# A four-bank burst for the first Fourier stage in a fused S4D and gated-GLU kernel

## The chip, the cores and the metric

The kernel runs on one core of one Trainium2 chip. The metric is device time in microseconds (us). Before the change, three runs gave 742.46, 738.54 and 740.25 us, a median of 740.25 us. One more execution was recorded by the hardware profiler, and all lines of profile and trace below come from that one.

The engines are named as the profile names them: PE is the matrix engine (PEld its weight loads), DVE the vector engine, ACT the scalar engine, POOL the GpSimd engine, SP the engine that here only issues transfers. ACTq and SPq stand for the transfer queues that ACT and SP feed. Every engine works through its own list of instructions in a fixed order.

## The reference, cut to what matters

The input is one sequence of 2048 tokens with 448 channels. After a layer norm, two branches are computed from the same normalized tokens and added to the input:

```
xn = layernorm(x)                                   # x: [1, 2048, 448]
# branch A: a state-space layer as one long convolution
K  = 2 * Re( sum_n C[d,n] * dt[d] * exp(A[d,n] * dt[d] * l) )     # 448 channels, 256 states, l < 2048
yA = irfft( rfft(xn, 4096) * rfft(K, 4096) )[:2048] + xn * D_skip
# branch B: a gated feed-forward layer, 448 -> 1792 -> 448
yB = (sigmoid(xn @ w_gate) * (xn @ w_up)) @ w_down
out = x + yA + yB
```

## The kernel before, in words

Two generators, `conv` (branch A) and `glu` (branch B), emit work in turn. Each `yield` returns a number of units, and the loop at the end of the kernel always continues the generator that has done the smaller share of its total. So the interleaving of the two branches is set by these numbers. After that a scheduler, which simulates a timeline, sets the final order of the instructions on every engine; a smaller change in one place can therefore move instructions elsewhere. `tc.issue_after(i)` holds an instruction back, in that order, until instruction `i` has been placed; `hp` gives priority.

Branch B is done in two halves of 1024 tokens, each half being two blocks of 512 tokens. The 1792 hidden units are cut into 14 tiles of 128, and the tiles into groups of 3, 3, 3, 3 and 2. For each tile and block, `gate` runs 22 matmuls (L693) into two PSUM banks called `gu`: 11 for the gate and 11 for the up projection, because each product of 32-bit numbers is split into high and low parts (`xh`, `xl`, `wh`, `wl`). ACT then takes the tanh (`th`, L701) from the first bank, DVE multiplies it with the second (`hf`, L704), ACT casts (`hh`, L709) and DVE subtracts (`hl`, L711). A new weight tile costs a load on SP (`wraw`), a cast on ACT (`wh`, L743) and a subtraction on DVE (`wl`, L747). When a group of tiles is through, eight output groups `po` (L806) run, one per 128 tokens, and DVE adds each to an accumulator (`acc`, L811). `gu` and `po` share one ring of four PSUM banks: a new `gu` or `po` waits until the bank that was used four places earlier has been read by ACT (`th`) or DVE (`hf`, `acc`).

Branch A first prepares its parameters (`prep`, two halves of 224 channels each: exponentials, reciprocals in pieces L317, arctan, sines, on DVE, ACT and POOL), stores them as phases `ph_d` in device memory, and then builds the convolution kernel in 56 chunks (`kgen`). Each chunk begins on PE with the two matmuls `tr<-sel,ph` (L526), goes through ACT (`S`, L532 to L535) and DVE (`Et`, `Ft`, L586 to L588) and returns to PE (`ko<-Et,Ft`, L600). While chunks are built, branch B fills the engines' free time. The last part, `spectra`, multiplies spectra and transforms back.

The change touches the first Fourier stage of the tokens of the first half. It runs once per pair of token blocks of 128, in `x_spec`, four times in all, between the steps of `prep`. A pair needs four row groups of 32 partitions (g = 0 to 3). For one row group `x_first_stage` runs two matmuls with 32 rows and 64 columns each, one for either block of the pair, into the two halves of one PSUM bank; PE records each such matmul twice. `x_spec` does the four row groups in two steps of two: two row groups go into the two banks of the PSUM tile `tr`, ACT copies both banks to one of three SBUF slots (x1a, x1b, x1c, used in turn; L292), and ACT's queue stores the slot with two transfers (L295). The tiles `tr` (two banks), `ko` and `kp` (one bank each) have one buffer each; `ko` and `kp` are otherwise used by the transposes of the prepared parameters (`turn`, L426) and, later, by the chunks. For the second half of the tokens, another function, `pair_first`, does the same stage in one go over four banks of the `gu` ring.

## Time and profile before

| what | value |
|---|---|
| median of three runs | 740.25 us (738.54 to 742.46) |
| profiled execution, its own time | 735.94 us |
| its span, first to last instruction | 734.2 us |
| mean granted PE clock | 0.978 of full speed |
| busy: PE, DVE, ACT, POOL | 682.4, 557.0, 421.1, 355.9 us |
| `x_spec`: bursts on PE | 8 in the trace, from 42.49 to 79.64 us |
| `prep`: last phase product on DVE (L403) | 107.27 us |
| first chunk on PE (L526) | 127.40 us |

Times in the rows of the trace are counted from the first instruction. A row of the timeline gives start, duration, engine, line, operation, destination and source, shapes and the number of merged instructions; square brackets give how long the engine had been idle and what ended the wait. A table of stretches gives, for each stretch, its length, the busy time of PE, PEld, DVE, ACT and POOL with the number of instructions, the granted PE clock, the busy share of the transfer engines, and GB/s. The profiled execution lies 4.31 us below the median of the runs.

### The profile page before, as it was taken

The page shows a single profiled execution, that of the slowest core. Times are in us where ns is not written, and L with a number is a line of the kernel's source. Part 1 is how long each engine was busy: PE and PEld are TensorE (multiplying, and loading weights), DVE is VectorE, ACT ScalarE, POOL GpSimd, SP SyncE. Part 2 cuts the span into 40 slices and gives each one's busy share as a digit, 9 for nine tenths or more (in the row PEclk, how much of TensorE's full clock was granted, in tenths as well). Part 3 has the DMA queues.
Part 4 walks back from the last instruction along what each step waited for, and adds up shares of the span by engine and source line. Part 5 has one row for each costly group of instructions (what it writes and reads, how often), then busy time and mean ns, then how long its engine had stood idle before and what let it go on. Part 6 is the DMA issues. An engine that isn't in the chain of part 4 may idle for free.

```text
span 734.2 us, 19242 instructions
## 1 busy us (share of the span) xinstructions
PE 682.4 (93%) x7780; PEld 532.7 (73%) x7780; DVE 557.0 (76%) x776; ACT 421.1 (57%) x650; POOL 355.9 (48%) x423
## 2 busy tenths in 40 slices
PE   2898998999999899999999999998999999999995
PEld 2666787877877687565888877887877778776784
DVE  5899995699978989768667987977975555565543
ACT  3646483578677868797487787677652222323320
POOL 2110055684975986548467498486855001441002
PEclk9999999999999999699999999999999999999998
DMA  9946445444324635345972332332158999999845
GB/s 208 225 131 179 113 135 176 134 138 168 96 89 135 221 86 155 98 127 174 278 191 88 111 108 80 100 104 80 45 163 272 257 253 241 266 262 221 199 118 160
DMA packets 102984, 117.24 MB, mean 160 GB/s; under 512 B 13232, under 2 KB 90864, under 8 KB 102896
## 3 DMA queue, kind: packets, MB, share of 16 engines
q1 hardware_dynamic: 78736, 91.87, 45.3%
q10 hardware_dynamic: 21584, 18.24, 9.6%
q0 software_dynamic: 2576, 5.90, 3.0%
q8 instruction: 61, 1.00, 0.6%
q14 instruction: 27, 0.22, 0.1%
HBM read 72.13 MB, written 43.84 MB: 158 GB/s over the span
## 4 chain that ended last, share of the span: by engine, by line
PE 55%; DVE 17%; ACT 8%; DMA 8%; issue 5%; POOL 4%; SPq 2%; ACTq 1%; DVEq 0%; POOLq 0%
PE gu L693 23%; PE po L806 13%; PE sp L888 5%; PE ko L600 5%; PE pv L915 3%; PE tr L526 3%; DVE Ft L588 2%; DVE Et L587 2%; ACT S L535 2%; DVE Et L586 2%; DVE pm L440 2%; ACT S L532 1%; DMA sx<-x_d 1%; ACT S L533 1%; DMA tb<-in_c_tab_dram 1%
## 5 line engine op out<-in xcount | busy, mean ns | idle before, releaser
L504 POOL TENSOR_TENSOR me<-me,pm 128x32 f32<-128x32 f32 (+1 forms) x168 | 137.5, 819 | 114.8 <-DVE Et L587 102.9
L504 POOL TENSOR_TENSOR mf<-mf,pm 128x64 f32<-128x64 f32 (+1 forms) x112 | 113.8, 1016 | 5.2
L693 PE MATMUL gu<-xh,wh 128*128 128x512 f32 x336 | 100.2, 404 | 2.6 <-DVE acc L811 1.1
L693 PE MATMUL gu<-xh,wl 128*128 128x512 f32 x336 | 97.8, 396 | 0.0
L693 PE MATMUL gu<-xl,wh 128*128 128x512 f32 x336 | 96.2, 394 | 0.0
L586 DVE TENSOR_TENSOR Et<-me,S 128x1024 f32<-128x1024 f32 x56 | 80.1, 1430 | 18.1 <-ACT S L535 17.0
L587 DVE TENSOR_TENSOR Et<-me,S 128x1024 f32<-128x1024 f32 x56 | 78.9, 1410 | 15.4 <-ACT me L517 12.0
L806 PE MATMUL po<-dh,hh 128*128 128x448 f32 x224 | 85.1, 380 | 3.7 <-DVE acc L811 3.0
L588 DVE TENSOR_TENSOR Ft<-mf,S 128x1024 f32<-128x1024 f32 x56 | 79.3, 1416 | 5.5 <-ACT S L535 4.5
L806 PE MATMUL po<-dl,hh 128*128 128x448 f32 x224 | 83.2, 371 | 0.0
L806 PE MATMUL po<-dh,hl 128*128 128x448 f32 x224 | 82.4, 369 | 0.0
L693 PEld LDWEIGHTS gu<-xh,wh 128*128 128x128 f32 x336 | 61.2, 190 | 23.5 <-issue 6.1
L600 PEld LDWEIGHTS ko<-Et,Ft 128*32 128x32 f32 x3584 | 54.5, 111 | 32.3 <-DVE Ft L588 13.8
L532 ACT ACTIVATE S<-tr 128x1024 f32<-128x1024 f32 x56 | 57.7, 1030 | 33.2 <-PE tr L526 31.5
L600 PE MATMUL ko<-Et,Ft 128*32 128x64 f32 x3584 | 64.9, 223 | 12.4 <-DVE Ft L588 12.4
L693 PEld LDWEIGHTS gu<-xh,wl 128*128 128x128 f32 x336 | 63.7, 190 | 14.7 <-DVE ys L257 0.7
L693 PEld LDWEIGHTS gu<-xl,wh 128*128 128x128 f32 x336 | 63.8, 190 | 14.3 <-issue 0.7
L709 ACT CAST hh<-hf 128x512 fp32r<-128x512 f32 x56 | 34.9, 623 | 62.7 <-DVE hf L704 62.6
L704 DVE SCALAR_TENSOR_TENSOR hf<-th,gu 128x512 f32<-128x512 f32 x56 | 38.2, 682 | 40.4 <-PE gu L693 34.7
L701 ACT ACTIVATE th<-gu 128x512 f32<-128x512 f32 x56 | 33.6, 601 | 59.6 <-PE gu L693 46.1
L535 ACT ACTIVATE S<-S,hpi 128x1024 f32<-128x1024 f32 x56 | 65.6, 1172 | 0.0
L811 DVE SCALAR_TENSOR_TENSOR acc<-po,acc 128x448 f32<-128x448 f32 x80 | 48.1, 617 | 19.4 <-PE po L806 19.4
(198 smaller groups left out, 1295.1 us busy)
## 6 DMA issues: line engine op xcount, KB each, us to landing
sk_d<-sk ACTq DMA_DIRECT2D x14, 512.0 KB
sx<-x_d SPq DMA_DIRECT2D x32, 224.0 KB
skl<-sk_d SPq DMA_DIRECT2D x16, 448.0 KB
vp<-v_d SPq DMA_DIRECT2D x16, 448.0 KB
v_d<-vt SPq DMA_DIRECT2D x62, 112.0 KB
ph<-ph_d SPq DMA_DIRECT2D x224, 24.0 KB
wt_d<-wh SPq DMA_DIRECT2D x9, 512.0 KB
wt_d<-wl SPq DMA_DIRECT2D x9, 512.0 KB
```

What stands on the lines that cost most here:

```text
L504: ins = nc.gpsimd.tensor_tensor(m[:, :, w + a : 2 * w : n], m[:, :, a:w:n], par(base + i).unsqueeze(2).to_broadcast([128, 4 * DC, w // n]) ...
L532: nc.scalar.activation(rows(cs), pv, AF.Abs)
L535: sins[:] = [nc.scalar.activation(cs, cs, AF.Sin, scale=-TWO_PI, bias=hpi)]
L586: v.tensor_tensor(Et[:, :, :, 32:64], two(me[:, :, 32:64]), S[:, 1::-1], ALU.mult)
L587: v.tensor_tensor(Et[:, :, :, 0:32], two(me[:, :, 0:32]), S[:, 1:3, :, ::-1], ALU.mult)
L588: fts[:] = [v.tensor_tensor(Ft, two(mf), S[:, 3:5], ALU.mult)]
L600: mm = nc.tensor.matmul(ko[32 * j : 32 * j + 32, sl], Ft[:, cc, DC * h + 4 * q + j], Et[:, cc, DC * h + 4 * q + j], start=(k == 0), stop=( ...
L693: glu_mm[:] = [nc.tensor.matmul(ps, a_, b_, start=(n == 0), stop=(n == len(mm) - 1))]
L704: marks[1] = v.scalar_tensor_tensor(hf, th, 1.0, pgu[1], ALU.add, ALU.mult)
L806: glu_mm[:] = [nc.tensor.matmul(po, a_[:, bs], w_, start=(n == 0), stop=(n == 3 * fc - 1))]
L811: v.scalar_tensor_tensor(acc[:, b], po, 0.5, acc[:, b], ALU.mult, ALU.add)
L888: mm = nc.tensor.matmul(to, tb[:kk, t, 64 * c : 64 * c + 64], rhs, start=True, stop=True, skip_group_check=True,)
```

## The change

`x_spec` now takes two slots at once and runs all four row groups in one burst: the first two into the two banks of `tr` as before, the third into `ko`, the fourth into `kp`. One copy moves the two banks of `tr` to the first slot; two copies of half the size move `ko` and `kp` to the two halves of the second slot. The four stores follow. The generator yields once, with twice the units, so that its total is unchanged. The slots are taken in the same turn: pairs (a, b), (c, a), (b, c), (a, b).

```
 def x_spec(xn, b0):
+    x1s_ = []
+    for _ in range(2):
+        x1s_.append(slots[("x1a", "x1b", "x1c")[x1s[0] % 3]])
+        x1s[0] += 1
+    ps = psc[-1].tile([128, 2, 512], F32, name="tr", bufs=1)
+    kk = [psc[-1].tile([128, 512], F32, name=n, bufs=1) for n in ("ko", "kp")]
+    with tc.issue_after(glu_mm[0].ins):
+        for j in range(4):
+            x_first_stage((ps[:, j] if j < 2 else kk[j - 2])[:, :D], xn, j)
+    nc.scalar.copy(x1s_[0], ps[:, :, :D])
+    for j in range(2):
+        nc.scalar.copy(x1s_[1][:, j], kk[j][:, :D])
     for p in range(2):
-        x1 = slots[("x1a", "x1b", "x1c")[x1s[0] % 3]]
-        x1s[0] += 1
-        ps = psc[-1].tile([128, 2, 512], F32, name="tr", bufs=1)
-        with tc.issue_after(glu_mm[0].ins):
-            for j in range(2):
-                x_first_stage(ps[:, j, :D], xn, 2 * p + j)
-        nc.scalar.copy(x1, ps[:, :, :D])
         for i in range(2):
             r = row(b0 + i, 2 * p)
-            nc.scalar.dma_start(x1_d[:, r : r + 9 : 8], x1[64 * i : 64 * i + 64])
-        yield WX
+            nc.scalar.dma_start(x1_d[:, r : r + 9 : 8], x1s_[p][64 * i : 64 * i + 64])
+    yield 2 * WX
```

The lines behind `x_spec` move down by five, so that L693, L806, L811, L317 and L526 of the profile are L698, L811, L816, L322 and L531 of the changed kernel. The scheduler then places instructions differently at three places that matter here. In the lists below, a row is a line, an operation, its destination and source, a shape and a count.

The first place is PE, from the first burst to the second (`tr`, `ko` and `kp` are the PSUM banks; `gu` are the matmuls of branch B's gates). Before:

```order
L281 MATMUL tr<-xn_117,wx 64x448 x4
L693 MATMUL gu<-xh,wh 128x512 x3
L693 MATMUL gu<-xr,wh 128x512
L693 MATMUL gu<-xh,wl 128x512 x3
L693 MATMUL gu<-xr,wl 128x512
L693 MATMUL gu<-xl,wh 128x512 x3
L693 MATMUL gu<-xh,wh 128x512 x3
L693 MATMUL gu<-xr,wh 128x512
L693 MATMUL gu<-xh,wh 128x512 x3
L693 MATMUL gu<-xr,wh 128x512
L281 MATMUL tr<-xn_117,wx 64x448 x4
```

These two bursts carry four row groups, with 19 gate matmuls between them. On the same engine, at the same place, now:

```order
L281 MATMUL tr<-xn_117,wx 64x448 x4
L281 MATMUL ko<-xn_117,wx 64x448 x2
L281 MATMUL kp<-xn_117,wx 64x448 x2
L698 MATMUL gu<-xh,wh 128x512 x3
L698 MATMUL gu<-xr,wh 128x512
L698 MATMUL gu<-xh,wl 128x512 x3
L698 MATMUL gu<-xr,wl 128x512
L698 MATMUL gu<-xl,wh 128x512 x3
L698 MATMUL gu<-xh,wh 128x512 x3
L698 MATMUL gu<-xr,wh 128x512
L698 MATMUL gu<-xh,wh 128x512
L281 MATMUL tr<-xn_117,wx 64x448 x4
```

One burst now holds all four row groups, and the next pair's burst follows after 16 gate matmuls.

The second place is DVE, in the first output groups of branch B: `acc` are their eight additions, of which the fifth and later ones stand here, and `pl`, `a`, `w` and `ex` belong to `prep`. Before:

```order
L412 TENSOR_TENSOR a_377<-a_377,b_378 112x512
L317 RECIPROCAL pl<-pl 112x128 x4
L259 TENSOR_TENSOR z<-ys 128x8
L811 SCALAR_TENSOR_TENSOR acc<-po,acc 128x448 x2
L412 TENSOR_TENSOR a_389<-a_389,b_390 112x512
L317 RECIPROCAL pl<-pl 112x128 x4
L377 SCALAR_TENSOR_TENSOR w_392<-ci,w_392 112x512
L811 SCALAR_TENSOR_TENSOR acc<-po,acc 128x448
```

The fifth addition stands behind four of the eight reciprocal pieces. On the same engine now:

```order
L259 TENSOR_TENSOR z<-ys 128x8
L382 SCALAR_TENSOR_TENSOR w_380<-ci,w_380 112x512
L417 TENSOR_TENSOR a_377<-a_377,b_378 112x512
L322 RECIPROCAL pl<-pl 112x128 x8
L816 SCALAR_TENSOR_TENSOR acc<-po,acc 128x448 x2
L417 TENSOR_TENSOR a_389<-a_389,b_390 112x512
L260 SCALAR_TENSOR_TENSOR z<-z,ve 128x8
L816 SCALAR_TENSOR_TENSOR acc<-po,acc 128x448 x2
```

Now it stands behind all eight pieces, and nothing else ahead of it has been removed.

The third place is PE, where the first chunk begins (`po` are the output groups of branch B's second group of tiles, 72 matmuls in all). Before:

```order
L806 MATMUL po<-dh,hl 128x448
L806 MATMUL po<-dh,hh 128x448
L806 MATMUL po<-dl,hh 128x448
L806 MATMUL po<-dh,hl 128x448
L806 MATMUL po<-dh,hh 128x448
L526 MATMUL tr<-sel,ph_1095 128x512 x2
```

At that point 264 gate matmuls and 112 output matmuls have been issued, 40 of them from the second group of tiles. On the same engine now:

```order
L698 MATMUL gu<-xl,wh 128x512 x3
L811 MATMUL po<-dh,hh 128x448
L811 MATMUL po<-dl,hh 128x448
L811 MATMUL po<-dh,hl 128x448
L811 MATMUL po<-dh,hh 128x448
L811 MATMUL po<-dl,hh 128x448
L811 MATMUL po<-dh,hl 128x448
L811 MATMUL po<-dh,hh 128x448
L811 MATMUL po<-dl,hh 128x448
L531 MATMUL tr<-sel,ph_1103 128x512 x2
```

The first chunk now comes after 264 gate matmuls and 80 output matmuls: 8 from the second group instead of 40. From the third chunk on, the same number of branch B's matmuls stands ahead of a chunk as before, up to shifts of a few matmuls, and of 35 at the thirtieth chunk.

## The prediction

> **What bounds the kernel now.** I first read the page's busy times, then the table of stretches around the change, then the timeline for who waits for whom. The first row is the page's engine line, the others are stretches (length, then busy time of PE, PEld, DVE, ACT, POOL).
>
> ```profile
> PE 682.4 (93%) x7780; PEld 532.7 (73%) x7780; DVE 557.0 (76%) x776; ACT 421.1 (57%) x650; POOL 355.9 (48%) x423
> ...
> 52.00:62.50 10.50, 9.48 (x54) 5.72 (x52) 10.50 (x15) 3.31 (x5) 1.62 (x1) 1.00 0.82 233
> 62.50:73.00 10.50, 9.11 (x46) 7.07 (x42) 10.50 (x22) 9.51 (x14) 0.00 (x0) 0.84 0.57 159
> 73.00:83.50 10.50, 9.64 (x52) 6.98 (x52) 10.50 (x21) 7.13 (x12) 0.20 (x1) 1.00 0.42 103
> 83.50:99.00 15.50, 15.46 (x70) 12.81 (x71) 15.50 (x30) 6.82 (x14) 1.16 (x1) 1.00 0.23 71
> 99.00:111.00 12.00, 12.00 (x59) 9.95 (x58) 11.53 (x14) 9.43 (x20) 11.71 (x5) 1.00 0.73 210
> 111.00:127.00 16.00, 13.04 (x61) 11.30 (x61) 7.98 (x14) 4.46 (x9) 7.55 (x14) 0.95 0.62 190
> 127.00:147.00 20.00, 20.00 (x146) 16.62 (x145) 12.64 (x18) 10.80 (x15) 14.13 (x19) 0.96 0.39 126
> 147.00:167.00 20.00, 19.84 (x206) 16.02 (x205) 18.38 (x17) 16.10 (x24) 16.44 (x17) 1.00 0.48 164
> 167.00:187.00 20.00, 17.59 (x313) 13.96 (x312) 19.03 (x26) 15.36 (x23) 10.24 (x13) 1.00 0.50 159
> 187.00:207.00 20.00, 19.75 (x270) 16.61 (x269) 16.75 (x15) 12.98 (x19) 19.15 (x19) 1.00 0.24 67
> 207.00:247.00 40.00, 34.82 (x553) 27.26 (x554) 35.54 (x38) 32.20 (x48) 25.55 (x31) 0.97 0.45 144
> ```
>
> Over the whole span PE is the bound (93%). But from 52 to 99 us, where the changed stage runs, DVE has no idle time at all, while PE stands still for 1.02, 1.39 and 0.86 us. There DVE, not PE, sets when things happen. From 127 to 167 PE is full; at 167 to 187 it idles 2.41 us, at 207 to 247 another 5.18.
>
> **The bursts on PE.** A burst of 8 records (two row groups), and bursts of 12 and 4 records of the same stage in the second half:
>
> ```profile
> 41.72 0.84 PE L693 MATMUL gu<-xl,wh 128*128 128x512 f32 x3
> 42.49 0.98 PE L281 MATMUL tr<-xn,wx 32*64 32x448 f32 x8
> 43.40 0.96 PE L693 MATMUL gu<-xh,wh 128*128 128x512 f32 x3
> 44.20 0.40 PE L693 MATMUL gu<-xr,wh 128*128 128x512 f32 x1
> ...
> 319.69 0.99 PE L281 MATMUL gu<-xt,wx 32*64 32x448 f32 x12
> 320.61 0.73 PE L526 MATMUL tr<-sel,ph 128*128 128x512 f32 x2
> 321.42 0.97 PE L281 MATMUL gu<-xt,wx 32*64 32x448 f32 x4
> ```
>
> 4, 8 and 12 records all take 0.97 to 0.99 us, so row groups run side by side, and I take 16 records at 0.98 too (bounds: 0.98, and 1.96 if the fourth row group does not join). A burst costs about 1.1 us: 0.91 from 42.49 to 43.40, 0.09 to 0.12 ahead of it (three matmuls of 0.227 after 41.72 end at 42.40), and the next three matmuls start their successor 0.80 instead of 0.68 later. Four bursts fewer are 4.4 us of PE, at the worst 0. Three of the eight lie after the wait at 63.26, and in the new order none.
>
> **What holds PE instead.** Waits of PE on DVE, and the DVE rows that end them:
>
> ```profile
> 62.52 0.69 DVE L704 SCALAR_TENSOR_TENSOR hf<-th,gu 128x512 f32<-128x512 f32 x1
> 63.26 0.47 PE L806 MATMUL po<-dh,hh 128*128 128x448 f32 x1 [0.71 <-DVE hf L704]
> ...
> 72.97 0.98 PE L281 MATMUL tr<-xn,wx 32*64 32x448 f32 x8 [0.68 <-ACT x1c L292]
> ...
> 79.54 3.40 DVE L317 RECIPROCAL pl<-pl 112x128 f32<-112x128 f32 x4
> 82.28 0.37 PE L806 MATMUL po<-dh,hl 128*128 128x448 f32 x1
> 82.86 1.16 DVE L811 SCALAR_TENSOR_TENSOR acc<-po,acc 128x448 f32<-128x448 f32 x2
> 83.54 0.73 PE L693 MATMUL gu<-xh,wh 128*128 128x512 f32 x2 [0.90 <-DVE acc L811]
> 84.52 3.40 DVE L317 RECIPROCAL pl<-pl 112x128 f32<-112x128 f32 x4
> ```
>
> At 63.26 PE waits for the bank that `hf` frees. DVE's work ahead of that `hf` is the same now but for one operation on 8 elements per partition, so PE gets there 3 us earlier and waits 3 us longer: nothing gained. At 83.54 the first gate of the next group of tiles waits for the bank of the fifth `acc`. In the new order four more reciprocal pieces stand ahead of that `acc` and nothing fewer. DVE has no idle time there to lose, so it ends 3.40 us later (84.52 row), and the gate starts at 86.94. It cannot be earlier unless DVE works faster; it can be later by what ACT adds, below. PE, 4.0 us ahead by three bursts of 1.1 and the 0.68 us that it waited for a copy at 72.97, then stands still for about 0.90 + 4.0 + 3.4 = 8.3 us instead of 0.90.
>
> **The clock.** What PE's clock did after waits:
>
> ```profile
> 64.00:67.00 3.00, 3.00 (x9) 2.67 (x8) 3.00 (x7) 2.79 (x4) 0.00 (x0) 0.50 0.43 127
> 125.70:128.60 2.90, 2.86 (x7) 2.48 (x8) 2.87 (x5) 1.14 (x2) 2.66 (x4) 0.50 0.20 56
> ```
>
> After the waits around 62 and before 125.70, PE ran about 3 us at half the clock, a loss of 1.5 us each; after the 0.90 us at 83.54 it did not (1.00 in both stretches there). With 8.3 us I take 1.5 us, bounds 0 and 1.5. The Trainium skill ("TensorE: Matmul & The Clock Gate", Part 1) says that the clock falls to half after an idle window of about 3.4 us and comes back after as much work. By that page the loss would be 1.7 us, an estimate from its window, and by its rule the shorter waits here should have cost nothing; the row at 64.00 disagrees on the latter. Gates thus run 4.9 us late: 3.4 + 1.5.
>
> **Copies, stores, slots.** One copy of 896 columns and, from the second half, two of 448:
>
> ```profile
> 43.54 0.91 ACT L292 COPY x1ab<-tr 128x896 f32<-128x896 f32 x1 [1.72 <-PE tr L281]
> 321.87 1.00 ACT L675 COPY x<-gu 128x448 f32<-128x448 f32 x2
> 44.48 0.68 ACTq L295 DMA_DIRECT2D x_d<-x1ab  x1
> 49.00:50.00 1.00, 1.00 (x5) 0.82 (x6) 1.00 (x3) 0.88 (x1) 0.00 (x0) 1.00 0.09 26
> L858 SPq DMA_DIRECT2D sx<-x_d x16: 580/612/1456, 532.1 to 677.6; - x16
> ```
>
> Four times 0.09 us more on ACT, hidden: ACT is busy 3.31 of 10.50 us at 52 to 62.5 and nearly full only at 62.5 to 73, where it could push `acc` back by at most some 1 us. The sixteen stores are the same and are read from 532 us on. New is that a copy can overwrite a slot whose stores were issued just before. The first stores, issued from 44.48 on, were through by 49 (transfer share 0.09 in that stretch), so such a copy waits up to some 4.5 us; the cast of tile 3's weights that is queued behind it on ACT is first needed by the gate at 83.54, so I cost it at nothing.
>
> **Where the first chunk starts.** The end of the gates and the first chunk:
>
> ```profile
> 115.32 0.36 PE L806 MATMUL po<-dh,hh 128*128 128x448 f32 x1
> 115.30:122.40 7.10, 7.10 (x36) 6.57 (x35) 1.78 (x6) 0.00 (x0) 1.57 (x6) 1.00 0.77 231
> 121.00 6.83 SPq L476 DMA_DIRECT2D ph<-ph_d  x16
> 125.74 0.74 PE L806 MATMUL po<-dh,hh 128*128 128x448 f32 x1 [2.96 <-DVE acc L811]
> 127.40 1.05 PE L526 MATMUL tr<-sel,ph 128*128 128x512 f32 x2
> ```
>
> Gates that ended at 115.32 now end at 120.2. Eight output matmuls (7.10/36 = 0.20 us each) bring PE to 121.8, and there it stands, in order, at the first chunk, which needs the loads of `ph`. These come at best 2.7 us earlier than before, since two `hf` and two `hl` of about 0.68 us fewer stand ahead of `prep`'s last operation on DVE, and at worst not earlier, because on SP they are queued behind the stores of tile 6, whose weights now load later. So the chunk starts between 124.7 and 127.4; I take 126.0. PE then still owes the 32 output matmuls that it had done by 127.40: 6.4 us. It is behind by 126.0 + 6.4 - 127.4 = 5.0 us, bounds 3.7 and 6.4.
>
> **What is given back.** From 127 to 167 PE is full, so it stays behind. At 167 to 187 its 2.41 us of idle time are waits for the chunk's chain on ACT and DVE, which now started 1.4 us earlier; a PE that is late finds the data ready. I take all of it, and nothing of the 5.18 us at 207 to 247, where DVE is busy 35.54 of 40 us, with work that also follows PE (bounds 0 and 7.6 in all). Sum: 3.4 + 1.5, then 5.0 at the first chunk, less 2.4: +2.6 us. Against the profiled execution, 735.94 becomes 738.5; against the median, which lies 4.31 above it, 740.25 becomes 742.8.
>
> **The rivals.** First, slower: nothing is given back, since chunks and gates are tied by one order on PE and all shift together. Then +5 to +6.4 us, 745.2 to 746.6. For it speaks that PE is full for 40 us after the first chunk; it decides if PE still idles some 2.4 us in the stretch that was 167 to 187. Second, faster: the lateness is regained entirely at 167 to 247, whose 7.6 us of idle time exceed it, and the earlier chunks (up to 2.7 us) shift the chain that ends last there. Then 737.5, or with the saved 4.4 us of PE all coming out 735.9. Against it, that chain also holds `hf` and `acc`, which follow PE. Third, the change doesn't do what it says: the four-bank burst takes twice as long. PE has some 8 us to spare at that place, so the time would be the forecast's, 742.8, within the same case.
>
> **How the numbers follow.** The forecast, with an end 0.5 to 3.7 us above the median before: 0.45. Nothing given back, or more lost: 0.37. Regained: 0.18, of which 0.03 end within 0.5%. The burst of twice the length (under 0.05) is part of the first. About 0.5% (3.7 us) is what a measurement of this kernel can tell from no change. So faster 0.15, same 0.48, slower 0.37. The likeliest case alone runs from 740.7 to 744.0; the range that leaves out 2 in 10 runs from 736.8, near the saved PE time coming out, to 748.0, which is 6.4 us late plus another half-clock stretch of 1.5.
>
> **What would show it.** Right: four bursts of 16 records of about 1 us; DVE still without idle time to 99 us; the gate of 83.54 at 87 or a little later behind a wait of some 8 us for `acc`, then half clock; PE waiting at the first chunk near 126. Given back: less than 1 us of PE idle where it had 2.41. Wrong: if that `acc` comes before 85 us, or if the chunks from 200 us on run earlier than before.

## The result, and the profile after

The changed kernel took 735.59 us (median of nine runs, 729.01 to 737.56) where the kernel before took 738.83 us in the same comparison (nine runs, 736.31 to 744.70). The ratio is 0.993, with a 95% interval of 0.9903 to 0.9957: it is 0.7% faster. (It is not the quotient of these two medians, which is 0.9956. Ratios below leave out disturbed runs, which are two of *rows1*, at 744.24 and 745.42 us, and one of the kernel before, at 748.66.) The prediction was 742.8 us, 2.6 us slower.

The profiled execution of the changed kernel took 737.56 us, its span is 735.7 us and its mean granted clock 0.974. So it is the longest of the nine, and 1.6 us longer than the profiled execution before; where that comes from is part of what follows. First the page's engine line and the table of stretches, both of the changed kernel, with the columns of the prediction's first fence. The row at 86.60 stands for a stretch of half clock, those from 280.60 on for places that the prediction did not speak of.

```profile
PE 680.4 (92%) x7780; PEld 535.5 (73%) x7780; DVE 560.1 (76%) x776; ACT 421.1 (57%) x654; POOL 360.6 (49%) x423
...
52.00:62.50 10.50, 9.08 (x63) 5.79 (x61) 10.50 (x17) 5.00 (x9) 2.26 (x2) 1.00 0.80 231
62.50:73.00 10.50, 8.84 (x30) 7.66 (x30) 10.23 (x21) 8.80 (x14) 0.00 (x0) 0.67 0.68 172
73.00:83.50 10.50, 7.57 (x36) 6.68 (x36) 10.50 (x20) 5.96 (x12) 0.00 (x0) 1.00 0.24 68
83.50:99.00 15.50, 11.54 (x41) 9.27 (x42) 15.07 (x32) 5.66 (x13) 1.61 (x2) 0.78 0.21 67
111.00:127.00 16.00, 16.00 (x77) 13.69 (x76) 8.81 (x17) 8.28 (x15) 9.09 (x16) 1.00 0.49 154
147.00:167.00 20.00, 19.88 (x206) 15.93 (x205) 15.85 (x16) 15.08 (x22) 9.03 (x11) 1.00 0.54 179
167.00:187.00 20.00, 19.85 (x325) 16.21 (x324) 19.90 (x26) 17.36 (x26) 13.04 (x14) 1.00 0.47 147
207.00:247.00 40.00, 34.99 (x615) 27.70 (x617) 36.71 (x39) 33.96 (x51) 32.16 (x32) 1.00 0.48 151
280.60:383.60 103.00, 97.05 (x1372) 68.72 (x1371) 80.49 (x96) 79.78 (x129) 64.22 (x81) 0.97 0.59 174
648.00:656.00 8.00, 5.33 (x78) 3.15 (x75) 7.93 (x12) 0.53 (x1) 4.25 (x4) 0.82 1.08 274
...
86.60:93.40 6.80, 5.94 (x14) 4.69 (x15) 6.80 (x19) 0.84 (x2) 0.00 (x0) 0.50 0.00 0
```

Up to 99 us PE stands for 1.42, 1.66, 2.93 and 3.96 us in the first four stretches, 10.0 us where it stood 3.3 before, and in two of them its clock is at half for a part. At 111 to 127 it does better than before: 16.00 us busy instead of 13.04, at full clock. At 167 to 187 the 2.41 us of idle time are down to 0.15. At 648 to 656 there is a new hole of 2.67 us.

The same two kernels in the time at which PE reaches the same instruction (this table is worked out from both traces by pairing equal matmuls in order, and counts the changed kernel less the kernel before; where chunks and branch B's work have moved against each other, between 147 and 285 us, the row names what is paired):

| place, by the clock of before | PE, us |
|---|---|
| end of the gates (115.32, now 122.02) | +6.7 |
| next gate behind the output groups (134.97, now 138.17) | +3.2 |
| 140 to 147 | +2.0 |
| 187 to 200, output groups | -0.5 |
| 285 to 300 | -2.6 |
| 384 to 480 | -4.2 |
| 490 to 648 | -3.9 |
| from 660 | +1.3 |

So the change is late by 6.7 us, is 3.9 us ahead by 490 us, and in this one execution loses 5.2 us at 650. The first part of the story is told by the timeline of the changed kernel: a burst, the waits of PE on DVE, and the first chunk.

```profile
42.71 0.60 PE L281 MATMUL tr<-xn,wx 32*64 32x448 f32 x4
42.75 0.59 PE L281 MATMUL kp<-xn,wx 32*64 32x448 f32 x2
...
43.17 0.54 PE L281 MATMUL kp<-xn,wx 32*64 32x448 f32 x2
...
64.16 0.74 PE L811 MATMUL po<-dh,hh 128*128 128x448 f32 x1 [3.07 <-DVE hf L709]
...
80.30 6.62 DVE L322 RECIPROCAL pl<-pl 112x128 f32<-112x128 f32 x8
86.85 1.09 DVE L816 SCALAR_TENSOR_TENSOR acc<-po,acc 128x448 f32<-128x448 f32 x2
...
87.46 1.65 PE L698 MATMUL gu<-xh,wh 128*128 128x512 f32 x3 [6.08 <-DVE acc L816]
...
112.49 1.11 SPq L633 DMA_DIRECT2D wraw<-in_B_w_up_dram  x2
115.37 1.05 ACT L748 CAST wh<-wraw 128x1024 fp32r<-128x1024 f32 x1 [4.75 <-DMA wraw<-in_B_w_up_dram]
116.45 1.23 DVE L752 TENSOR_TENSOR wl<-wraw,wh 128x1024 fp32r<-128x1024 f32 x1 [3.89 <-DMA rd<-in_B_w_down_dram]
118.12 7.82 SPq L481 DMA_DIRECT2D ph<-ph_d  x16
122.02 0.36 PE L811 MATMUL po<-dh,hh 128*128 128x448 f32 x1
123.64 0.63 PE L531 MATMUL tr<-sel,ph 128*128 128x512 f32 x2
```

The burst of four row groups takes 1.00 us (43.17 + 0.54 - 42.71). The first gate of the next group of tiles comes at 87.46, behind all eight reciprocal pieces, and the gates end 6.7 us late. But the first chunk stands at 123.64 with no wait before it: it comes 3.76 us earlier than before. Three more profiles whose PE order is the same here (*again*, *wl_dve* and *wl_pieces*, below) have it at 123.73 to 124.63, each with a wait of 0.96 to 1.48 us for ACT's `hh` just ahead of it. In *again*:

```profile
123.00 0.47 PE L811 MATMUL po<-dh,hh 128*128 128x448 f32 x1 [1.48 <-ACT hh L714]
123.73 0.90 PE L531 MATMUL tr<-sel,ph 128*128 128x512 f32 x2
```

The kernel before, in the same 15 us:

```profile
118.74 1.54 SPq L628 DMA_DIRECT2D wraw<-in_B_w_up_dram  x2
...
122.65 1.04 ACT L743 CAST wh<-wraw 128x1024 fp32r<-128x1024 f32 x1 [8.53 <-DMA wraw<-in_B_w_up_dram]
123.73 1.22 DVE L747 TENSOR_TENSOR wl<-wraw,wh 128x1024 fp32r<-128x1024 f32 x1 [6.54 <-DMA ph<-ph_d]
125.07 0.62 DVE L811 SCALAR_TENSOR_TENSOR acc<-po,acc 128x448 f32<-128x448 f32 x1
```

The wait of 2.96 us that the prediction quotes at 125.74 is named for `acc`. But DVE had stood idle for 6.54 us, at the subtraction `wl` of tile 7, whose weights had been loaded by SP as late as 118.74, behind the stores of `ph_d`; the `acc` that PE needed stood behind that `wl`. In the changed order SP issues this load between the stores, the last piece at 112.49, the cast and `wl` come 7.28 us earlier, and the wait for `acc` is gone, with its half clock.

### The profile page after: what moved, and what is told of

The parts are those of the page before. It is cut to its first block, busy times and chain, and to the rows that moved or that the text cites. A ratio compares the mean times of both kernels' runs of the same rounds, so it can differ in the third digit from the quotient of the medians.

```text
span 735.7 us, 19244 instructions
## 1 busy us (share of the span) xinstructions
PE 680.4 (92%) x7780; PEld 535.5 (73%) x7780; DVE 560.1 (76%) x776; ACT 421.1 (57%) x654; POOL 360.6 (49%) x423
## 4 chain that ended last, share of the span: by engine, by line
PE 63%; DVE 13%; DMA 7%; ACT 7%; issue 4%; SPq 3%; POOL 1%; ACTq 1%; POOLq 0%; DVEq 0%
PE gu L698 29%; PE po L811 11%; PE sp L893 7%; PE ko L605 5%; PE pv L920 4%; PE tr L531 3%; DVE Et L591 2%; DVE Ft L593 2%; DVE Et L592 2%; SPq L633 1%; ACT S L540 1%; ACT S L538 1%; DVE acc L816 1%; SPq L481 1%; DMA t<-in_c_t_dram 1%
## 5 line engine op out<-in xcount | busy, mean ns | idle before, releaser
L509 POOL TENSOR_TENSOR me<-me,pm 128x32 f32<-128x32 f32 (+1 forms) x168 | 140.3, 835 | 107.4 <-DVE Et L592 96.3
L509 POOL TENSOR_TENSOR mf<-mf,pm 128x64 f32<-128x64 f32 (+1 forms) x112 | 118.2, 1056 | 4.7
L698 PE MATMUL gu<-xh,wh 128*128 128x512 f32 x336 | 102.3, 412 | 7.0 <-DVE acc L816 6.1
L698 PE MATMUL gu<-xh,wl 128*128 128x512 f32 x336 | 98.9, 402 | 0.0
L698 PE MATMUL gu<-xl,wh 128*128 128x512 f32 x336 | 97.5, 396 | 0.0
L591 DVE TENSOR_TENSOR Et<-me,S 128x1024 f32<-128x1024 f32 x56 | 82.8, 1479 | 12.5 <-ACT S L540 10.8
L592 DVE TENSOR_TENSOR Et<-me,S 128x1024 f32<-128x1024 f32 x56 | 79.4, 1417 | 12.3 <-ACT me L522 9.6
L811 PE MATMUL po<-dh,hh 128*128 128x448 f32 x224 | 85.0, 380 | 3.9 <-DVE hf L709 3.1
L698 PEld LDWEIGHTS gu<-xh,wh 128*128 128x128 f32 x336 | 63.2, 195 | 28.9 <-DVE acc L816 6.5
L811 PE MATMUL po<-dl,hh 128*128 128x448 f32 x224 | 83.0, 371 | 0.0
L811 PE MATMUL po<-dh,hl 128*128 128x448 f32 x224 | 82.0, 369 | 0.0
L593 DVE TENSOR_TENSOR Ft<-mf,S 128x1024 f32<-128x1024 f32 x56 | 76.8, 1372 | 5.2 <-ACT S L540 2.7
L698 PEld LDWEIGHTS gu<-xh,wl 128*128 128x128 f32 x336 | 65.1, 194 | 15.2 <-DVE pl L316 0.7
L698 PEld LDWEIGHTS gu<-xl,wh 128*128 128x128 f32 x336 | 64.5, 192 | 14.0
L816 DVE SCALAR_TENSOR_TENSOR acc<-po,acc 128x448 f32<-128x448 f32 x80 | 48.0, 614 | 21.7 <-PE po L811 21.7
```

The lines of the kernel that those rows point to most:

```text
L509: ins = nc.gpsimd.tensor_tensor(m[:, :, w + a : 2 * w : n], m[:, :, a:w:n], par(base + i).unsqueeze(2).to_broadcast([128, 4 * DC, w // n]) ...
L591: v.tensor_tensor(Et[:, :, :, 32:64], two(me[:, :, 32:64]), S[:, 1::-1], ALU.mult)
L592: v.tensor_tensor(Et[:, :, :, 0:32], two(me[:, :, 0:32]), S[:, 1:3, :, ::-1], ALU.mult)
L593: fts[:] = [v.tensor_tensor(Ft, two(mf), S[:, 3:5], ALU.mult)]
L698: glu_mm[:] = [nc.tensor.matmul(ps, a_, b_, start=(n == 0), stop=(n == len(mm) - 1))]
L811: glu_mm[:] = [nc.tensor.matmul(po, a_[:, bs], w_, start=(n == 0), stop=(n == 3 * fc - 1))]
```

## The experiments

Three explanations of the gain were set against each other: that the PE time saved by the bursts comes out in the end (Theory A of the expectations), and its rivals, that it is the wait removed at the first chunk (Theory B), or the different order further on (Theory C; in the expectations of *first_four* and *second_four* Theory B stands for the order behind the stage). The diffs are against the changed kernel or the kernel before, as named.

### Is it the saved PE time?

**again**: the changed kernel, whose generator yields its units in two steps again. The order on all engines is the same.

```
-        yield 2 * WX
+        yield WX; yield WX
```

> The changed kernel with its one yield of 2*WX written as two of WX; every engine's order of instructions is the same as in the changed kernel. It gives a second profile of that order. The first profile of it (735.7 us of span) was 4.2 us ahead of the old kernel from 400 us on, 3.9 us ahead at 648, and lost 5.2 us between 648 and 662, where a DVE addition of 0.39 us took 2.43 us beside POOL's wl subtraction, PE waited 2.67 us for it and then ran at half clock for 6.8 us. If this collision is a matter of the moment at which a weight load lands, some profiles lack it: then the span is near 730 us and PE has no wait of over 1 us between 640 and 660. If it belongs to the order, it is there again, with a span near 735. Median of the times in both cases 735.6, within 1.5.

736.11 us (733.29 to 738.79), ratio 0.996 (0.9935 to 0.9985). The gain is there with the units returned either way. Its profile is 4.2 us ahead by 480 us, 3.3 at 648 us, and has no hole at 650. (The opposite, one yield of twice the units in the kernel before, is the run *old_again* below.)

**rows2** and **rows1**: the changed kernel, with the four matmul pairs of a burst put on two row groups of PE, or on one, so that they cannot run side by side. In both, all banks but the first hold another row group's product. The edit of *rows2*; in *rows1* the map is `lambda g: 0`:

```
-    def x_first_stage(to, xn, g):
-        s = slice(32 * g, 32 * g + 32)
+    def x_first_stage(to, xn, g, m=lambda g: g):
+        s = slice(32 * m(g), 32 * m(g) + 32)
...
-                x_first_stage((ps[:, j] if j < 2 else kk[j - 2])[:, :D], xn, j)
+                x_first_stage((ps[:, j] if j < 2 else kk[j - 2])[:, :D], xn, j, lambda g: g // 2)
```

> The changed kernel, but the first two row groups of a burst both use row group 0 and the last two row group 1 (token data of a wrong group go into two of four banks, so the computation is changed there). Order of instructions the same on all engines. Matmuls of one row group run one after the other, so a burst should take about 2 us instead of 0.94, four bursts some 4 us more: the PE time that the change saved is put back, and nothing else. Theory A, the gain is PE's saved time: 735.6 + 4 = 739.6. Theory B, the gain comes from what moved on the other queues (the weights of the tile ahead of the first chunk landing 6 us earlier, so that the wait of 2.96 us at 125.74 and its half clock are gone): 735.6, since the waits of PE of 3.07 us (at 64.16) and 6.08 us (at 87.46) take up the 4 us.

> As the run with two row groups, but all four banks of a burst use row group 0 (the computation is changed in three of four banks). A burst of 16 records should take about 4 us, four of them 12 us more than in the changed kernel. Theory A: 735.6 + 12 = 747.6. Theory B: the two waits of 3.07 and 6.08 us take up 9 of the 12 us, 735.6 to 738.6, and the gates still start near 87.5, behind the fifth acc.

Beside *again*, in the same comparison, neither is slower by more than the intervals: 736.19 us, ratio 0.9956 (0.9925 to 0.9986), and 736.66 us, ratio 0.9959 (0.9932 to 0.9986). The timeline of *rows1*, a burst and PE's wait for `acc`:

```profile
40.89 1.72 PE L281 MATMUL tr<-xn,wx 32*64 32x448 f32 x8
42.45 0.92 PE L281 MATMUL ko<-xn,wx 32*64 32x448 f32 x4
43.20 0.92 PE L281 MATMUL kp<-xn,wx 32*64 32x448 f32 x4
...
90.22 1.65 PE L698 MATMUL gu<-xh,wh 128*128 128x512 f32 x3 [6.07 <-DVE acc L816]
```

A burst takes 3.23 us there (40.89 to 44.12), so the four cost 8.9 us more PE time (4 x 2.23) than the changed kernel's, twice what the change had saved. The gate that was expected near 87.5 starts at 90.22. At 648 us *rows1* is 1.7 us ahead of the kernel before, 2.2 behind the changed one. By these two profiles a us of burst on PE costs a quarter of a us, 2.2 of 8.9. This is a rough estimate, since the profiles of the changed kernel, *again*, *wl_dve* and *wl_pieces* lie 2.9 to 5.3 us ahead there with the same bursts. Theory A, which asked for 747.6 us, falls: of 4.4 us saved, some 1 us can come out.

**first_four** and **second_four**: four-bank bursts for the first two pairs alone, or for the last two alone; the others go through the old function, here `x_spec2`. The edit of *first_four*; *second_four* has `n == 3`:

```
-                            yield from x_spec([xns[n - 2][:, b + i] for i in range(2)], 4 * (n - 2) + b)
+                            yield from (x_spec if n == 2 else x_spec2)([xns[n - 2][:, b + i] for i in range(2)], 4 * (n - 2) + b)
```

> The burst over four banks for the first four token blocks alone; the second four run as in the old kernel, in two bursts over two banks. Two bursts fewer instead of four: 2.2 us of PE saved. PE's order from its 545th matmul on (about 145 us) is that of the changed kernel but for three rows. Theory A (what comes out is PE time saved): half the gain, 737.4 against 739.1 and 735.9. Theory B (what comes out is the new order of the work behind the stage): the whole gain, 735.9, with the half-clock stretch near 296 us of 6.8 us that the changed order has in all three profiles so far.

> The burst over four banks for the second four token blocks alone. Again 2.2 us of PE saved, but PE's order from 145 to about 285 us is that of the old kernel, and from there to 360 us a third one. Theory A: half the gain, 737.4. Theory B: no gain from 145 to 285 us, where the changed order gained 3 us against the old one; about 738.5, unless the third order behind 285 us has its own gain or loss, of 1.7 us for every half-clock stretch of 3.4 us more or less than the 13.65 us of the old one.

*first_four*: 735.25 us, ratio 0.9953 (0.9929 to 0.9977), with two bursts saved instead of four: the whole gain and not half of it, as Theory B of its expectation had it. *second_four*: 736.39 us, ratio 0.9972 (0.9945 to 1.0000). In its trace the third and fourth bank of a burst were placed apart from the first two, so that it has eight bursts as before and saves no PE time in them; it is 2.9 us ahead at 126 us all the same, and 4.4 at 383. That agrees with the row-group runs.

### Is it the wait at the first chunk?

**load_first**: the kernel before, with one weight load given priority. It was meant for tile 7 and moved tile 6's.

```
-                            raw, rd = raws.pop() if raws else (w_load(f), None)
+                            with hp(HP if f == 6 else 0):
+                                raw, rd = raws.pop() if raws else (w_load(f), None)
```

> The old kernel with one thing moved: the loads of the weights of tile 6 have a higher priority and are issued on SP ahead of the last ph_d stores instead of behind them. Bursts and banks as before. In the old profile these loads went out from 115.61 on, their cast came at 122.65, DVE stood still for 6.54 us until 123.73, and PE waited 2.96 us at 125.74 and ran at half clock until 128.6. Theory B: the load goes out some 3 us earlier, the cast comes near 119 to 120, PE's wait and its half clock (1.4 us) are gone, and the time falls by 2 to 4.4 us, to 734.4 to 737 against 738.8. Theory A, only the PE time of the bursts counts: no change, 738.8, since other waits take the place of this one.

738.08 us, ratio 0.9978 (0.9952 to 1.0004). Tile 7's load was still late, but on DVE the `acc` came to stand ahead of the waiting `wl`: PE's wait for `acc` at 125 was gone, two shorter ones of 0.35 and 1.15 us came, and PE was 2.5 us ahead at 133 us. By 343 us 0.9 were left, at 490 to 648 us nothing.

**tile7_act**: the kernel before, with tile 7's weights loaded by ACT's queue, past the stores on SP.

```
-                            raw, rd = raws.pop() if raws else (w_load(f), None)
+                            raw, rd = raws.pop() if raws else (w_load(f, eng=nc.scalar if f == 7 else nc.sync), None)
```

> The old kernel with the weights of tile 7 (those loaded from 115.61 us on in its profile; the run before that moved a load had moved tile 6's) loaded through ACT's queue instead of SP's, where they stood behind the last ph_d stores. Their buffer is free at 109.4, so they can go out some 5 us earlier. PE's order is the old one but for three matmuls. Theory B (step 5 of the prediction failed because PE's wait at 125.74 hung on this load): the cast comes near 117 to 119 instead of 122.65, the DVE wait of 6.54 us shrinks to 1 to 3 us, the PE wait of 2.96 us and the half clock at 125 are gone, and at 134 us PE is 2 to 4 us ahead of the old profile. The time: of that lead some 2 us were left at 285 us in the two kernels with the old order that had it, so 736.5 to 738 against 738.5. If the lead at 134 is below 1 us, the wait hung on something else (the loads of ph, from 121.0).

737.76 us, ratio 0.9973 (0.9946 to 1.0001). This kernel waits at the first chunk, for the load of `ph`, instead of for `acc`:

```profile
124.56 0.70 PE L526 MATMUL tr<-sel,ph 128*128 128x512 f32 x2 [1.53 <-DMA ph<-ph_d]
```

2.96 us of wait and 1.5 us of half clock went, 1.53 us came: 2.9 us by the sum, 2.6 us by the pairing of matmuls, the same from 133 to 260 us. That is as much as the changed kernel has at 285 us, had from the old bursts by moving one load, but the changed kernel gets there in another way, as the text behind *old_again* shows. Behind 341 us 0.95 us of it were left.

**old_again**: the kernel before with one yield of twice the units; the order is that of before.

```
-            yield WX
+        yield 2 * WX
```

> The old kernel with its yield of WX behind each of the two bursts written as 2*WX; the order of instructions is the same on every engine. A second profile of the old order: if the 13.65 us of half clock from 296 us on belong to the order, they are there again within 3.4 us (the changed order had 6.8 there in six profiles, with 3.4 more at 329 in four of these), and so are the wait of 2.96 us of PE at 125.74 and the one of DVE ahead of it. Median 738.5, within 1.5.

739.17 us, ratio 0.9974 (0.9948 to 1.0000); in its profile PE waits 2.93 us for `acc` at 125.42, DVE 6.53 us for tile 7's cast, as before. The wait belongs to the old order, not to one execution.

The removed wait can't be the whole gain: the changed kernel is still 2.0 us late at 140 us and 2.6 us ahead by 285 to 300. From 147 to 285 us, eight kernels have one and the same order on PE, matmul for matmul (the changed kernel, *again*, *rows1*, *rows2*, *first_four*, and *wl_dve*, *wl_pieces* and *late_old* below), and the ten others that of before, but for four matmuls in one of them. By the same pairing, from 140 to 147 until 285 to 300 us, the eight regain 4.6 to 6.3 us on the kernel before, whether PE is 1.8 us late at 140 us or, in *late_old*, 21.8. The nine others range from 2.3 us lost to 1.4 us gained. So this part of the gain belongs to the changed order; it needs neither saved PE time nor a first chunk that is early by the clock (127.24 us in *rows1*, 138.60 in *late_old*). What in that order brings it is not shown.

### What lies between 285 and 383 us?

In this stretch *tile7_act* lost 1.8 us of its lead and *load_first* 1, while the changed kernel gained some 1.4. From the 20th to the 33rd `Ft` row (280.6 to 383.6 us before), the six profiles whose order there is that of before take 102.9 to 106.4 us, mean 104.4 (the kernel before, old_again, load_first, tile7_act, and late_old and wl_pieces_old below). Eight kernels with four-bank bursts, whose order there is another, take 99.8 to 102.3 us, mean 101.1 (the changed kernel, again, rows1, rows2, first_four, second_four, and wl_dve and wl_pieces below). These lengths are worked out from the traces. The stretch of the kernel before, and a row of its timeline:

```profile
280.60:383.60 103.00, 98.27 (x1365) 68.64 (x1364) 78.80 (x96) 79.04 (x126) 63.20 (x80) 0.93 0.61 172
...
314.09 0.41 PE L212 MATMUL gu<-ident,xt 128*64 128x128 f32 x2 [0.91 <-DVE xl L222]
```

The clock is 0.93 where the changed kernel has 0.97: half clock for 13.7 us, after for 6.8. PE waits at 314.09 at a transpose of tokens of the second half (L212) for a DVE operation, in *old_again* 2.17 us. In the order before, that transpose stands ahead of a chunk and the `Ft` matmuls (L600) right behind it; in the changed order a whole gate (310.37 to 312.9) stands there, and PE doesn't wait.

**late_old**: the changed kernel with each four-bank burst done twice, so that no PE time is saved.

```
-            for j in range(4):
+            for j in (0, 1, 2, 3) * 2:
                 x_first_stage((ps[:, j] if j < 2 else kk[j - 2])[:, :D], xn, j)
```

> The changed kernel with every burst of 16 records done twice, so that PE's time is again that of the old kernel (the second burst computes the same data once more). Its order is that of the changed kernel from about 145 to 285 us and that of the old one from there on. Theory C, the gain is made between 285 and 325 us, where the changed order stood at half clock for 6.8 instead of 13.65 us: the time is 738.5 to 739. Theory B without C, the gain is made before 285 us: 736 to 736.7. In the trace: lead over the old kernel at 280 us 1 to 3 us as in the changed order, and whether it grows by the 3.4 us of the clock until 325 us.

756.16 us, ratio 1.025 (1.0216 to 1.0285): a miss as a test of the early part, since the scheduler made an early order of its own, in which PE waits 3.30 us for a copy, 4.83 and 2.91 at two more places and 9.52 us for an `acc` at 99.73. From 278 us on its order is that of before, and it stays 16.2 us late there, 16.1 at the end of the stretch. With the old late order nothing is gained in the stretch, however late PE comes.

**turn_late** and **both_waits**: the kernel before, with the transposes of two pairs moved back; *both_waits* has the load of *tile7_act* as well.

```
-            for b in range(nb):
+            with hp(-HP if nb == 2 and k == 3 and o0 == 256 else 0):
+                for b in range(nb):
...
```

> The old kernel with the two bursts over two banks, but the last transposes (64 columns) of the pairs 10 and 14 without their raised priority, so that PE comes to them behind the matmuls of the next chunk instead of ahead of them. In the old order PE waits there, near 313 us, for DVE's xl (0.91, 2.17, 2.12, 2.66, 3.48 us in five profiles); in the changed order these transposes stand later and there is no wait. Between the 20th and the 33rd Ft row that DVE shows (280.6 and 383.6 us in the old profile) six profiles of the old order took 102.9 to 106.4 us, on the mean 104.4, and eight of other orders 99.8 to 102.3, on the mean 101.1. Theory C, a good half of the change's gain is this later order: the stretch takes 100 to 102.3 here too, and the time falls by some 2 to 3.5 us, to 735.5 to 737.5 against 739. If the stretch still takes 103 us or more, the wait near 313 only hid another one.

> The old kernel and its eight bursts, with both moves: tile 7's weights loaded through ACT's queue (PE 2.58 us ahead at 134 us when it was alone) and the 64-column transposes of the pairs 10 and 14 later. If the change's gain consists of these two waits and not of the PE time of its bursts, the old bursts have it too: lead over the old profile 2 to 3 us at 280, 4 to 6 us at 383, and a time of 734 to 736 against 739. If a part hangs on the bursts themselves, it stays above 737.

Both missed. 742.42 us, ratio 1.0042 (1.0017 to 1.0068), and 738.95 us, ratio 1.0003 (0.9979 to 1.0028). The wait at the transpose went and a longer one stood behind it, in *turn_late*:

```profile
316.00 0.42 PE L601 MATMUL ko<-Et,Ft 128*32 128x64 f32 x2 [3.05 <-DVE Ft L589]
```

The stretch took 109.2 us in *turn_late* and 108.0 in *both_waits*, with some 20 us of half clock in either.

**gate_between** and **gate_elsewhere**: the kernel before, with one gate of branch B given priority, so that six of its matmuls stand between chunk and `Ft` matmuls, or a gate that doesn't come to stand there. The edit of *gate_between*; *gate_elsewhere* has `n_ == 1`:

```
-            with tc.issue_after(order[0].ins) if order else nullcontext():
+            with tc.issue_after(order[0].ins) if order else nullcontext(), (hp(HP) if soon == i else nullcontext()):
...
-                    yield from gate(ws[f - f0], xq[2 * half + t], hs[t], between, half == 0 and (f, t) == (1, 0))
+                    yield from gate(ws[f - f0], xq[2 * half + t], hs[t], between, half == 0 and (f, t) == (1, 0), 1 if cross and n_ == 2 else None)
```

> The kernel before, with one of branch B's gates of the group in which the second half begins (third tile of the group, second block) placed with priority, so that 6 gate matmuls stand on PE between the matmuls that open a chunk and the Ft matmuls that follow, near 313 us. Theory: it is the gate at that place, there in the changed order and not in the order before, that covers PE's wait near 313 us; then the stretch from the 20th to the 33rd Ft row takes 101 to 102.5 us where the old order took 103 to 106, the half-clock time there falls to 7 us or less, and the time is some 2 us shorter (ratio near 0.997). Rival: the wait depends on more than that gate (the earlier start of everything from 125 us on, or where the 64-column transposes stand); then the stretch stays at 103 us or more and the ratio at 1.00 or above. Moving the gate also moves POOL's work on the second half, which could lengthen the stretch by itself.

> The same move, with priority for the gate of the second tile instead of the third, so that no gate comes to stand between the chunk and the Ft matmuls near 313 us. Theory (the covering gate): the stretch from the 20th to the 33rd Ft row takes 104 to 109 us, ratio 1.00 or above. Rival (any earlier gate does it): 101 to 102.5 us, as with the other gate.

741.57 us, ratio 1.002 (0.9995 to 1.0045), stretch 103.6 us; and 744.38 us, ratio 1.005 (1.0029 to 1.0071), stretch 108.3 us. In *gate_between* the gate stands where it should, and PE waits all the same:

```profile
316.87 0.52 PE L600 MATMUL ko<-Et,Ft 128*32 128x64 f32 x18 [0.80 <-DVE Ft L588]
318.25 0.41 PE L212 MATMUL gu<-ident,xt 128*64 128x128 f32 x2 [0.85 <-DVE xl L222]
```

So one gate at that place is not the cause. Which part of the changed order shortens the stretch stays open. The stretch is short in all eight profiles with a new order there (six have one and the same, *first_four* and *second_four* variants of it), and no single move of the old order brought it.

### What is the hole at 650 us?

The changed kernel at its new hole (`wl` is the second half's weight subtraction, on POOL; `yy` and `pd` belong to `spectra`, and both inputs of L907 lie in SBUF):

```profile
648.43 1.04 POOL L758 CAST wh<-wraw 128x1024 fp32r<-128x1024 f32 x1 [6.20 <-PE sp L893]
...
649.55 2.37 POOL L759 TENSOR_TENSOR wl<-wraw,wh 128x1024 fp32r<-128x1024 f32 x1
649.74 2.43 DVE L907 TENSOR_TENSOR yy<-pd 128x224 f32<-128x224 f32 x1
...
653.38 1.72 PE L955 MATMUL pv<-vp,wf 64*32 64x224 f32 x16 [2.67 <-DVE pd L905]
...
653.99 0.38 DVE L907 TENSOR_TENSOR yy<-pd 128x224 f32<-128x224 f32 x1
```

The same DVE operation takes 0.38 us at 653.99 and 2.43 us beside POOL's subtraction, and ends 0.25 us after it. PE, two operations further, waits 2.67 us, and then runs 6.8 us at half clock. The rule of the Trainium skill ("SBUF — State Buffer", "Who interferes with whom") is that a DVE instruction with two inputs in SBUF contends with a GpSimd instruction that reads SBUF, and it calls this contention an exclusive lock; these rows agree, with a DVE operation that lasts as long as POOL's. Three more profiles have this hole or one of 0.76 us (*rows2*, *second_four*, *first_four*), *again* and *rows1* have none. It depends on when POOL's subtraction falls: in *again* it starts at 651.12, behind the first of these DVE operations (0.39 us), and holds the second (2.04 us), for which PE doesn't wait. In the kernel before, POOL's subtraction came at 657.93, with DVE past these operations.

**wl_dve**: the changed kernel, with these subtractions on DVE.

```
-                            nc.gpsimd.tensor_tensor(wl, raw, wh, ALU.subtract)
+                            v.tensor_tensor(wl, raw, wh, ALU.subtract)
```

> The changed kernel, but in the second half the five wl subtractions that POOL does (2.36 us each) are done by DVE (1.2 us each), which has 40 to 50% idle time there. If what parts the profiles by 5 us at 650 us is that a DVE operation stands behind POOL's wl subtraction (2.43 instead of 0.39 us), it is in none of its executions: no wait of PE of over 1 us from 640 to 660, no half clock there, times without the upper group, and a median of some 733 to 734 against 735.9. If the slow group has another cause, the median stays at 735.9 and both groups remain; if DVE comes to be late with its own work, above 737.

739.15 us, ratio 1.0016 (0.9990 to 1.0042): a miss. DVE works in order too, and now waits for POOL's cast:

```profile
652.68 1.23 DVE L759 TENSOR_TENSOR wl<-wraw,wh 128x1024 fp32r<-128x1024 f32 x1 [5.45 <-POOL wh L758]
...
655.12 3.51 PE L955 MATMUL pv<-vp,wf 64*32 64x224 f32 x48 [4.20 <-DVE pd L905]
```

**wl_pieces** and **wl_pieces_old**: the subtraction on POOL in four pieces, in the changed kernel and in the kernel before.

```
-                            nc.gpsimd.tensor_tensor(wl, raw, wh, ALU.subtract)
+                            for k in range(4):
+                                nc.gpsimd.tensor_tensor(wl[:, :, k], raw[:, :, k], wh[:, :, k], ALU.subtract)
```

> The changed kernel; in the second half POOL does each of its five wl subtractions in four pieces of a quarter, some 0.6 to 0.7 us each instead of 2.36. All other engines keep their order. If DVE operations with two inputs wait for a running POOL subtraction to end, they now wait for a piece at most: none takes over 1.2 us near 650 us where 0.39 to 0.61 is its own time, PE does not wait over 1 us there, the half clock behind it is gone, and the upper group of times (736 to 739) goes: median 732 to 734 against 735.6 to 736.1 of the undivided version. If the pieces follow each other without a gap that lets DVE in, DVE waits 2 to 3 us as before and the median stays near 735.8.

> The old kernel with the same division of POOL's wl subtractions. Its profile had no such wait of PE near 650 us, but its times spread from 735 to 748 us, so others of its executions may have it. If so, the median falls by 1 to 3 us, to 735.5 to 737.5; if the wait belongs to the changed order alone, it stays near 738.5.

*wl_pieces*: 733.85 us, ratio 0.9913 (0.9879 to 0.9946), the fastest of the study. *wl_pieces_old*: 741.55 us, ratio 1.0001 (0.9976 to 1.0026). The changed kernel with pieces, at the same place, by the timeline and the table of stretches:

```profile
649.87 2.99 POOL L760 TENSOR_TENSOR wl<-wraw,wh 128x256 fp32r<-128x256 f32 x4
...
650.49 0.39 DVE L908 TENSOR_TENSOR yy<-pd 128x224 f32<-128x224 f32 x1
...
648.00:656.00 8.00, 7.96 (x88) 5.80 (x72) 4.52 (x10) 0.60 (x1) 5.72 (x8) 1.00 0.97 275
```

The four pieces take 2.99 us and the DVE operation among them 0.39. PE is busy 7.96 of 8.00 us, and the lead of 5.3 us at 648 us in this profile is kept. In the kernel before, with no such collision at that place, the pieces bring nothing. So a DVE operation among the pieces is not held, and without its delay PE has no hole. That the pieces remove the hole from every execution is not shown, since *again* and *rows1* have none without them; nor that they make the changed kernel faster on average, since 0.9913 and 0.993 lie within each other's intervals. Nor are the upper times gone, as the expectation had it: the seven runs reach 739.73 us.

## Why the prediction was wrong

The prediction had PE late for good, by 2.6 us at the end; it ended some 4 us ahead before the hole at 650, and the median of 735.59 us lies 1.2 us below its range. Of the 6.8 us between +2.6 and the -4.2 at 384 to 480 us, 3.0 arise at the first chunk and 3.8 behind it. By its own steps:

- **The bursts on PE**: right. Four bursts of 16 records at 1.00 us; up to the same matmul (653.50 us before, 649.60 now) PE's busy time fell from 611.5 to 606.5 us, at equal time of half clock. The runs *rows1* and *rows2* show that hardly any of it is worth something in the end, as it said.
- **What holds PE instead**: right. PE waits 3.07 us for `hf` (the forecast was 3 us longer than 0.71), and the gate foretold for 86.94 came at 87.46, behind a wait of 6.08 us where 8.3 were foretold; most of the rest had gone into the longer half clock behind 64.16 (6.8 us from 62.68 on, 3.4 before). DVE was full but for 0.27 and 0.43 us.
- **The clock**: the mechanism was right, and the term too small for the profiled execution. 1.5 us was taken, the top of its bounds; the half clock after 87.46 lasted 6.8 us (the 0.50 row at 86.60), and the gates went from 3.9 us late to 6.7, so it cost 2.8 us. By the estimate from the Trainium skill ("TensorE: Matmul & The Clock Gate", Part 1) it would have been 1.7 us, one window; here it was two. In *again*, *wl_dve* and *wl_pieces* the same gates lost 1.3, 1.8 and 2.4 us, with half clock of 6.8 us in each, but from 83.11, 84.35 and 85.69 us on instead of 86.57: the more of it fell into PE's wait, the less it cost.
- **Copies, stores, slots**: right. PE waits for no copy of this stage in the changed kernel.
- **Where the first chunk starts**: this is the first of two steps that failed. It had PE reach the first chunk and stand there until 126.0 for the loads of `ph`, at worst until 127.4, "because on SP they are queued behind the stores of tile 6, whose weights now load later", and PE behind by 5.0 us (3.7 to 6.4). Measured: the chunk at 123.64 without a wait, outside the bounds of 124.7 to 127.4, and PE behind by 2.0 us; in *again*, *wl_dve* and *wl_pieces* the chunk at 123.73 to 124.63, behind the shorter wait for `hh`, and PE behind by 3.0 to 3.8. In none of them does it wait for `ph`. The step looked at the loads of `ph` on SP and took the 2.96 us at 125.74, whose row it quoted, for nothing that could go. That wait was a weight load on the same queue, tile 7's, passed on through ACT's cast and DVE's order, and the changed order moves this load in among the stores. The sum with that term agrees for the profiled execution: 6.7 us late, less 2.96 of wait, less 1.5 of half clock, is 2.2.
- **What is given back**: the second step that failed, and the larger part of the miss. Its 2.4 us at 167 to 187 came out, 2.5 measured (+2.0 to -0.5). Of the reason that it gave, a late PE that finds the data ready, lateness alone is not enough: *gate_between*, with the order of before and PE 1.75 us late at 140 us, has won back nothing by 185 us. The chunks that start earlier against PE's other work remain possible: the second chunk stands at 133.42 instead of 139.98 us. That this part of the number came out may thus be luck. The "nothing of the 5.18 us" behind it was wrong in effect: 2.1 us more came by 285 to 300 us, and another 1.6 us by 384, in the stretch that the order shortens, though PE's idle time at 207 to 247 fell only from 5.18 to 5.01. The runs show in its place that the changed order regains 4.6 to 6.3 us from 140 to 300 us, however late PE is; the prediction had no term for that. What in the order brings it stays open.
- **The rivals**: the faster one was nearest. The lateness is regained, as it said, though not out of the idle time that it named: PE's 7.6 us at 167 to 247 fell by 2.4. Its other reason, "the saved 4.4 us of PE all coming out", is refuted by *rows1*. The slower one fell with the idle time that was regained at 167 to 187. The prediction had named chunks from 200 us on that run earlier than before as the sign that it was wrong, and they do, by 1.7 us at the first and some 3 us by 285.
- Not foreseen at all: the hole at 650 us, which costs 5.2 us in the profiled execution and hides the gain there.

## What to carry to other kernels

A wait is named for the instruction that came last, but an engine that works in order passes on older delays: before a wait on DVE is taken as given, look at what DVE itself waited for, down to the queue of the transfer, and ask whether the new order moves that transfer. Time saved on the busiest engine is worth little where it waits for another one a moment later; an experiment that adds twice the saved time again shows its worth. Where a scheduler sets the order, a small change can bring a new order far behind it, and that order can be worth more than the change: profiles of kernels that share the order, and of others that don't, tell the two apart. And an earlier chain can meet a collision that it used to miss: cutting a long GpSimd operation into pieces is worth a try where the vector engine's operations with two inputs from SBUF lie beside it.

## What was not expected of the hardware

Stretches of half clock on PE had lengths of 3.4, 6.8, 10.2 or 13.7 us in the traces, multiples of 3.4, but for the last one of each trace, and one of 6.8 us followed a wait of 2.67 us. Four row groups side by side take 1.00 us, all four on one row group 3.23 us. A DVE addition of 0.38 us took 2.43 us beside a GpSimd subtraction of 2.37 us, and 0.39 us when that one was cut into four.
